# Fifteen loads moved to ScalarE's queue and a new fixed order in a recurrent-attention and maxout-FFN kernel

## The chip, the cores and the metric

The kernel runs on one core of a Trainium2 chip. A core has a matrix engine (PE, TensorE), a vector engine (DVE, VectorE), an activation engine (ACT, ScalarE), a general engine (POOL, GpSimd) and a sync engine (SP), each with its own instruction queue that runs in order. Transfers are issued by SP or ACT and carried out by 16 DMA engines. The metric is device microseconds of one execution, the median over several runs.

## The reference

Thirty-two heads (4 batches of 8) run a gated linear recurrence over 768 steps with head width 48; the result is laid out as 3072 tokens of 384 features and goes through an FFN with a maximum of three products.

```python
state = zeros(B, H, 48, 48)
for t in range(768):
    state = alpha[:, :, t, :, None] * state + einsum('bhd,bhe->bhde', k[:, :, t], v[:, :, t])
    y[:, :, t] = einsum('bhd,bhde->bhe', q[:, :, t], state)
x = y.transpose(0, 2, 1, 3).reshape(3072, 384)
h = maximum(maximum(x @ w1, x @ w2), x @ w3)      # [3072, 768]
out = h @ w_out                                   # [3072, 384]
```

Inputs and output are 32-bit; the kernel computes in 16-bit with 32-bit sums.

## The kernel before

**Tiling.** Time is cut into 6 chunks of 128 steps. One chunk of one batch is a *unit* u (24 in all, all 8 heads of 128 tokens); two units form a *group* n (12 in all). Within a unit the recurrence becomes products of matrices: logarithms of alpha (ln) are summed by a triangular product (cums), exponentials of the sums (ep, en) scale q and k (q~, k~), which are turned by PE (turn, copied back as qkT) or by a DMA transpose (cross, for the units in CROSS_Q). Scores of a unit are masked (LA), multiplied by v and added to the carried state's part (outs), scaled (xb) and turned into the FFN's layout (x turn and xT, or cross x for the units in CROSS_X). The state goes on by sums, U, G and Z.

**FFN.** max(x w1, x w2, x w3) w_out is computed as x (w1 w_out) plus max(relu(x (w2-w1)), x (w3-w1)) w_out. So w1 is cast (cast 0), turned (w1 turn) and multiplied by w_out (fold, w1o), and two differences are formed (sub 1, sub 2). For units u0 and u0+1, "grow u0 q g" is a product with difference g+1 for a part q of the 768 features, "relu" (ACT) and "max" (DVE) evict it, and "shrink m" gives the output of unit m, which is copied (ob) and stored. "zeros" are 27 products of zeros that fill PE at the start.

**Loads.** Each group has four loads (a, k, q, v) of 384 KB in runs of 192 bytes; the first four groups are loaded in halves of 192 KB, named "load x n 0" and "load x n 8". There are four buffers of each kind (LOADED), so the load of group n waits for the readers of group n-4. The four weight matrices come in two pieces each ("weights g 0" of 384 KB, "weights g 1" of 768 KB).

**The fixed order.** Nothing is scheduled while it runs. `Plan.step` (lines 135 to 157) records 801 steps with what each reads and writes, and `Plan.issue` (lines 159 to 167) emits them in the order written out in ORDER; each step goes to the first engine in its list of options, or to the second where PICK has its number. BANKS names the PSUM bank of each product's result. Since each engine runs its instructions in order, ORDER is five orders in one: the order among steps on one engine counts, and an instruction that waits holds all those behind it on its engine. SP's queue of the old order has 90 steps: 64 loads, 8 pieces of weights, 11 transposes and 7 stores; ACT's queue has 176 instructions of arithmetic and 18 stores. The options of a load stand in `load_options` (line 109), where only SP is named.

Of the kernel before, what the change touches and what calls it, by code (L numbers as in the profile page):

```python
# [35 lines left out]
    4, 5, 6, 0, 8, 9, 65, 2, 82, 1, 83, 84, 85, 10, 86, 64, 34, 88, 123, 3, 92, 89, 68, 7, 127,  # L36
    69, 94, 90, 70, 11, 71, 129, 128, 72, 32, 131, 74, 37, 91, 130, 66, 75, 133, 76, 134, 109,
    135, 35, 12, 116, 36, 136, 112, 87, 14, 56, 77, 73, 119, 132, 42, 97, 95, 106, 137, 120, 54,
    138, 78, 110, 104, 79, 33, 13, 139, 111, 80, 52, 115, 105, 121, 96, 101, 99, 93, 45, 40,
    124, 39, 81, 57, 122, 281, 44, 15, 140, 67, 98, 55, 141, 38, 102, 113, 292, 142, 103, 143,  # L40
    144, 277, 53, 288, 342, 282, 346, 289, 114, 43, 16, 117, 107, 145, 108, 20, 147, 100, 347,
    125, 148, 41, 17, 149, 293, 62, 150, 343, 60, 47, 18, 63, 146, 22, 58, 61, 278, 151, 283,
    46, 21, 126, 155, 294, 23, 59, 166, 152, 344, 48, 28, 156, 284, 279, 167, 24, 290, 168, 280,
    180, 153, 170, 345, 157, 181, 285, 154, 182, 19, 169, 158, 159, 295, 183, 233, 172, 357,
    291, 25, 163, 49, 160, 358, 296, 184, 286, 26, 173, 51, 185, 50, 161, 186, 164, 297, 174,
    162, 187, 348, 165, 175, 353, 31, 171, 195, 188, 359, 194, 30, 189, 29, 354, 176, 355, 177,
    360, 219, 190, 221, 356, 205, 178, 196, 207, 349, 118, 361, 27, 206, 191, 220, 179, 197,
    237, 192, 198, 350, 299, 209, 193, 234, 208, 415, 224, 287, 211, 416, 202, 417, 212, 222,
    235, 203, 407, 204, 418, 236, 362, 223, 199, 213, 408, 411, 300, 214, 210, 298, 225, 351,
    409, 412, 200, 413, 201, 226, 410, 263, 215, 303, 414, 238, 249, 227, 422, 264, 228, 265,  # L50
    251, 364, 267, 216, 250, 301, 323, 315, 229, 239, 253, 217, 419, 423, 218, 302, 252, 230,
    240, 317, 266, 231, 245, 255, 324, 232, 254, 365, 269, 246, 256, 241, 268, 471, 270, 247,
    325, 475, 242, 316, 248, 366, 271, 420, 243, 257, 425, 473, 272, 476, 327, 477, 368, 485,
    258, 244, 304, 273, 319, 472, 467, 478, 274, 388, 259, 318, 367, 474, 469, 260, 380, 326,
    275, 305, 261, 468, 321, 306, 262, 329, 352, 276, 369, 381, 470, 307, 530, 328, 320, 322,
    534, 370, 363, 330, 311, 531, 479, 312, 535, 308, 382, 309, 331, 390, 384, 526, 332, 310,
    427, 482, 392, 527, 333, 480, 383, 389, 426, 536, 421, 488, 313, 334, 429, 486, 537, 391,
    386, 532, 335, 387, 314, 441, 528, 533, 443, 336, 371, 338, 424, 529, 394, 339, 372, 541,
    395, 483, 489, 393, 373, 374, 396, 337, 542, 340, 442, 398, 376, 538, 487, 444, 341, 375,
    377, 448, 585, 544, 450, 397, 378, 589, 481, 385, 379, 593, 452, 590, 399, 445, 449, 430,  # L60
    403, 400, 594, 447, 451, 501, 595, 404, 431, 586, 587, 428, 596, 401, 405, 432, 591, 546,
    402, 406, 484, 588, 433, 651, 503, 592, 539, 647, 505, 502, 434, 437, 508, 648, 454, 504,
    600, 652, 506, 455, 510, 438, 507, 513, 456, 512, 548, 643, 439, 545, 458, 509, 440, 603,
    597, 543, 435, 605, 457, 644, 436, 540, 653, 601, 511, 645, 654, 446, 560, 649, 453, 646,
    561, 459, 563, 650, 490, 463, 491, 514, 604, 464, 658, 515, 460, 598, 562, 461, 516, 462,
    465, 492, 517, 567, 655, 602, 569, 466, 564, 568, 709, 571, 493, 518, 570, 547, 705, 710,
    566, 497, 607, 701, 494, 707, 706, 498, 599, 495, 573, 702, 711, 499, 708, 496, 703, 712,
    500, 519, 704, 626, 522, 520, 549, 619, 523, 627, 713, 521, 550, 628, 551, 621, 661, 630,
    524, 552, 620, 663, 556, 565, 716, 714, 662, 557, 622, 525, 553, 572, 629, 574, 656, 558,
    719, 632, 717, 575, 554, 659, 727, 555, 720, 721, 623, 576, 577, 723, 559, 625, 578, 665,  # L70
    581, 579, 725, 582, 606, 728, 664, 580, 608, 583, 729, 609, 584, 724, 610, 684, 741, 730,
    657, 745, 726, 742, 743, 722, 746, 747, 685, 744, 737, 686, 687, 748, 660, 615, 677, 734,
    688, 678, 616, 679, 690, 738, 680, 611, 633, 681, 612, 739, 634, 613, 683, 731, 614, 624,
    740, 631, 715, 636, 617, 718, 666, 635, 618, 752, 637, 667, 638, 732, 668, 689, 673, 639,
    753, 733, 749, 735, 640, 674, 641, 691, 750, 642, 675, 669, 682, 693, 755, 676, 736, 763,
    754, 670, 697, 765, 692, 671, 698, 757, 764, 672, 759, 766, 699, 694, 760, 700, 761, 695,
    756, 789, 751, 696, 758, 785, 790, 791, 762, 786, 787, 770, 788, 792, 767, 771, 773, 768,
# [685 lines left out]
```

## Time and profile before

| | |
|---|---|
| median of 3 runs | 152.29 us (152.26 to 152.42) |
| span of the profiled execution | 466.5 us |
| PE, matmuls | 1683, 457.5 us busy |
| DVE | 112.5 us busy, 196 instructions |
| ACT | 90.1 us busy, 177 instructions |
| POOL | 48.0 us busy, 72 instructions |
| DMA | 31.07 MB in 116131 packets |

The profiled execution took 466.5 us from its first to its last instruction, three times as long as the timed runs. Durations of single instructions, their order and their numbers can be read from it; which engine waits for which in the timed runs cannot be read from it directly. "PEld" is the loading of PE's weights, beside the matmuls; "SPq" and "ACTq" are the queues in which these engines issue transfers; an arrow "<-" names what ended an idle time.

### The profile page before, as it was taken

To read this page: it belongs to the slowest core of one execution; us is meant where nothing else is said; L and a number is where in the kernel's file an instruction comes from. 1 tells how busy PE (TensorE), PEld (TensorE's weight loads), DVE (VectorE), ACT (ScalarE), POOL (GpSimd) and SP (SyncE) were. 2 spreads that over 40 slices of the span, in tenths; PEclk is the share of its full clock that TensorE was granted. 3 is DMA by queue.
4 is the path that set the end of the run, shared out by engine and by line. 5 is a ranking of instruction groups with operands and counts; after the bars stand their busy time and mean duration, and the time that the engine had idled before them with its cause. 6 is when DMAs were issued, how large, how long until landed. Compare 5 with 4: busy or idle time off the path is not lost.

```text
span 466.5 us, 4171 instructions
## 1 busy us (share of the span) xinstructions
PE 457.5 (98%) x1683; PEld 263.5 (56%) x1683; DVE 112.5 (24%) x196; ACT 90.1 (19%) x177; POOL 48.0 (10%) x72
## 2 busy tenths in 40 slices
PE   4999999999999999999999999999999999999997
PEld 1667556674555656547546645545546554567473
DVE  5420313131123122222412221322221321231100
ACT  4323221122121312111212200121220111001010
POOL 0110002003001030210111120011110020000000
DMA  9999500540087000700032640020550030100001
GB/s 179 272 287 209 110 0 1 111 76 1 0 163 124 1 0 18 152 17 35 0 60 49 141 91 9 2 62 0 112 112 17 18 79 25 35 0 25 1 34 34
DMA packets 116131, 31.07 MB, mean 67 GB/s; under 512 B 109712, under 2 KB 114960, under 8 KB 116112
## 3 DMA queue, kind: packets, MB, share of 16 engines
q1 hardware_dynamic: 113232, 27.27, 27.9%
q10 hardware_dynamic: 2880, 3.54, 2.2%
q8 instruction: 13, 0.21, 0.2%
q14 instruction: 6, 0.05, 0.0%
HBM read 23.69 MB, written 4.72 MB: 61 GB/s over the span
## 4 chain that ended last, share of the span: by engine, by line
PE 98%; DMA 1%; SPq 0%; DVE 0%; issue 0%; DVEq 0%
PE psum L638 38%; PE psum L674 29%; PE psum L479 6%; PE psum L495 4%; PE psum L582 4%; PE psum L541 3%; PE psum L438 3%; PE psum L568 3%; PE psum L600 3%; PE psum L538 2%; PE psum L379 2%; DMA qn<-in_q_dram 1%; PE psum L362 1%; PE psum L408 1%; SPq L304 0%; DVE qk L450 0%
## 5 line engine op out<-in xcount | busy, mean ns | idle before, releaser
L638 PE MATMUL psum<-xT,wd 128*128 128x256 f16 (+1 forms) x540 | 186.4, 602 | 0.0
L638 PEld LDWEIGHTS <-wd 128*128 128x128 f16 x540 | 105.1, 209 | 67.5 <-issue 61.5
L674 PE MATMUL psum<-wo,hT 128*128 128x384 f16 (+1 forms) x150 | 96.7, 887 | 0.0
L674 PEld LDWEIGHTS <-hT 128*128 128x128 f16 x150 | 34.4, 230 | 54.6 <-issue 52.0
L674 PE MATMUL psum<-w1o,xT 128*128 128x384 f16 (+1 forms) x75 | 50.1, 847 | 0.0
L654 DVE TENSOR_TENSOR hT<-psum,hT 128x512 f16<-128x512 f32 (+1 forms) x39 | 24.7, 647 | 99.7 <-PE psum L638 99.7
L649 ACT ACTIVATE hT<-psum 128x512 f16<-128x512 f32 (+1 forms) x39 | 21.7, 564 | 111.0 <-PE psum L638 111.0
L500 DVE TENSOR_TENSOR LA<-psum,c 128x1024 f16<-128x1024 f32 x24 | 28.9, 1221 | 41.0 <-PE psum L495 28.7
L541 PE MATMUL psum<-v,LA 128*128 128x48 f16 x192 | 30.3, 314 | 0.0
L541 PEld LDWEIGHTS <-LA 128*128 128x128 f16 x192 | 26.5, 179 | 5.7 <-issue 5.1
L613 POOL TENSOR_TENSOR Z<-U,G 48x192 f16<-48x192 f32 x26 | 14.1, 543 | 109.5 <-DVE U L607 108.5
L438 PE MATMUL psum<-la,c 128*128 128x384 f16 x24 | 19.9, 847 | 4.3 <-ACT la L398 4.3
L479 PE MATMUL psum<-c,qk 128*128 128x128 f16 x96 | 22.1, 480 | 1.7 <-DVE qk L450 1.7
L479 PEld LDWEIGHTS <-qk 128*128 128x128 f16 x96 | 16.9, 208 | 9.1 <-DVE qk L450 4.0
L450 POOL TENSOR_TENSOR qk<-qn,ep 128x384 f16<-128x384 f32 x11 | 10.9, 994 | 105.2 <-ACT ep L443 94.0
L674 PEld LDWEIGHTS <-xT 128*128 128x128 f16 x75 | 13.1, 185 | 14.7 <-issue 14.2
L582 PE MATMUL psum<-Z 128*128 128x384 f16 x27 | 20.2, 869 | 0.0
L443 ACT ACTIVATE ep<-psum 128x384 f32<-128x384 f32 x24 | 11.7, 494 | 41.3 <-PE psum L438 41.2
L689 ACT COPY ob<-psum 128x384 f32<-128x384 f32 (+1 forms) x18 | 8.3, 469 | 54.7 <-PE psum L674 54.7
L554 DVE TENSOR_SCALAR xb<-psum,c 128x384 f16<-128x384 f32 x15 | 9.2, 617 | 37.9 <-PE psum L541 37.9
L568 PE MATMUL psum<-c,xb 128*128 128x128 f16 x63 | 17.5, 455 | 0.0
L446 ACT ACTIVATE en<-psum 128x384 f32<-128x384 f32 x24 | 11.5, 490 | 28.4 <-PE psum L438 27.1
(61 smaller groups left out, 297.2 us busy)
## 6 DMA issues: line engine op xcount, KB each, us to landing
out_dram<-ob ACTq DMA_DIRECT2D x17, 192.0 KB, 1.9
an<-in_alpha_dram SPq DMA_DIRECT2D x8, 384.0 KB, 5.3
kn<-in_k_dram SPq DMA_DIRECT2D x8, 384.0 KB, 5.4
qn<-in_q_dram SPq DMA_DIRECT2D x8, 384.0 KB, 5.7
vn<-in_v_dram SPq DMA_DIRECT2D x8, 384.0 KB, 4.2
ws<-in_moe_w_dram SPq DMA_DIRECT2D x3, 768.0 KB, 6.7
an<-in_alpha_dram SPq DMA_DIRECT2D x8, 192.0 KB, 4.0
kn<-in_k_dram SPq DMA_DIRECT2D x8, 192.0 KB, 4.0
```

The costliest lines, as they stand in the source:

```text
L438: nc.tensor.matmul(live[Lk], tri, la[:, hs, :D], start=True, stop=True)
L479: nc.tensor.transpose(live[tk][:, w, j, :], qk[:, w, 2 * j:2 * j + 2, :], ident)
L495: nc.tensor.matmul(live[Ak][:, p, j * P:(j + 1) * P], qkT[rows, 1, j, :], qkT[rows, 0, j, :], start=True, stop=True)
L500: lambda e: nc.vector.tensor_mul(LA.rearrange("p a b t -> p (a b) t"), live[Ak].rearrange("p a (b t) -> p (a b) t", t=P), maskA.unsqueeze( ...
L541: nc.tensor.matmul(yp[:, 2 * j + p, :], LA[:, p, j, :], v16[:, 2 * j + p, :], start=(cb == 0), stop=True, skip_group_check=True)
L568: nc.tensor.transpose(live[xk][:, ft, :], xb[:, ft * P:(ft + 1) * P], ident)
L582: nc.tensor.matmul(live["wm"], zero[:, :P], zero, start=True, stop=True)
L613: lambda e, rows=rows, cols=cols: engines[e].tensor_mul(Zn[rows, :, cols], (Us[u % 3] if cb else live[pk])[rows, :, cols], G[rows, i * NP: ...
L638: nc.tensor.matmul(live[gk][:, jj, :], wd[:, kt, g, j * P:(j + 1) * P], xT[:, kt, :], start=(kt == 0), stop=(kt == NFT - 1))
L649: lambda e, h=h, gk=gk: nc.scalar.activation(out=h, in_=live[gk], func=AFT.Relu),
L654: lambda e, h=h, gk=gk: nc.vector.tensor_max(h, live[gk], h),
L674: nc.tensor.matmul(live[ok][:, cols], a[:, i * P:(i + 1) * P], w[:, cols], start=(kt == 0), stop=(kt == nk - 1))
```

## The change

Loads get a second option, ACT, and a new order was written out with it: of the 801 places of ORDER 773 hold another step, of the 251 banks 215 are others, and PICK has 82 entries instead of 84. The steps themselves, their number and what they compute are the same, and PE's 273 steps keep their 1683 matmuls.

```diff
@@ ORDER, BANKS, PICK @@
 ORDER = (
-    4, 5, 6, 0, 8, 9, 65, 2, 82, 1, 83, 84, 85, 10, 86, 64, 34, 88, 123, 3, 92, 89, 68, 7, 127,
+    4, 8, 9, 5, 6, 0, 10, 12, 34, 7, 32, 1, 11, 2, 123, 65, 127, 82, 84, 128, 129, 83, 64, 131,
...
 PICK = {
-    44: 1, 71: 1, 72: 1, 75: 1, 79: 1, 81: 1, 85: 1, 86: 1, 120: 1, 131: 1, 132: 1, 145: 1, 146:
+    27: 1, 30: 1, 44: 1, 71: 1, 72: 1, 75: 1, 85: 1, 86: 1, 87: 1, 132: 1, 138: 1, 140: 1, 144:
...
 def load_options(share, n):
-    return [("SP", HARD, 0, HARD_LOAD * share, HARD_LATE * (n >= LATE_FROM))]
+    return [("SP", HARD, 0, HARD_LOAD * share, HARD_LATE * (n >= LATE_FROM)), ("ACT", 0.45, 0, HARD_LOAD * share)]
```

What the numbers come to, by the names of the steps:

- **Fifteen loads go to ACT's queue:** "v 3 0", "q 3 8", "q 4", "k 6", "v 6", "q 7", "v 7", "q 8", "a 9", "v 9", "k 10", "q 10", "v 10", "k 11" and "v 11". All stand behind the weights.
- **Stores:** six go from SP to ACT (units 0, 6, 10, 11, 20, 21) and three from ACT to SP (4, 12, 13).
- **Arithmetic:** 82 steps change their engine. Net, ACT has 7 more of them, DVE 10 fewer and POOL 3 more.
- **SP's first loads:** before a, k, q of unit 1, then a of unit 0, a and k of unit 2, q of 0, k of 0, q of 2, "weights 0 1", v of 0, 1, 2, "weights 0 0", "weights 1 1", a of unit 3, "weights 1 0", q of 3, "weights 3 1", k of 3, "weights 3 0", "weights 2 1", v of 3, "weights 2 0". After: a of unit 1, a and k of 2, k and q of 1, a of 0, q of 2, a of 3, "weights 0 1", v of 1, "weights 0 0", k of 0, v of 2, q of 0, "weights 1 0", "weights 1 1", v of 0, "weights 3 1", k and q of 3, "weights 3 0", "weights 2 1", "weights 2 0", then a of unit 4 and v of 3.
- **PE's order:** the products of one unit are spaced differently. Around unit 10 before: outs 10, turn 12, grow 8 1 1, cums 14, grow 8 0 1, x turn 10, outs 11. After: outs 11, outs 10, scores of 12 and 13, x turn 11, x turn 10.

118 rows, old and new, of tables (BANKS, ORDER, PICK) are left out of this document.

## The prediction

> **What bounds the kernel now.** I read the list of cores first, then the page (busy times, DMA, chain), then the timelines of the SP and ACT queues, the waits of SP, the groups by line, and last both orders in the code.
>
> ```profile
> core 0: 466.5 us, clock 1.000
> PE 457.5 (98%) x1683; PEld 263.5 (56%) x1683; DVE 112.5 (24%) x196; ACT 90.1 (19%) x177; POOL 48.0 (10%) x72
> PE 98%; DMA 1%; SPq 0%; DVE 0%; issue 0%; DVEq 0%
> 193.62 5.51 PE psum L674 x9
> DMA packets 116131, 31.07 MB, mean 67 GB/s; under 512 B 109712, under 2 KB 114960, under 8 KB 116112
> 20.00:50.00 30.00, 30.00 (x120) 19.92 (x118) 5.06 (x6) 9.56 (x17) 2.63 (x2) 1.00 1.07 249
> ```
>
> The profiled execution is not like the timed ones: its span is 466.5 us, the runs' median 152.29 us, a ratio of 0.326. Nine matmuls of 384 columns take 5.51 us, 612 ns each, though the granted clock reads 1.000. PE's 457.5 us must fit into 152.29, so in the runs PE is at least 3.0 times as fast, and what this profile calls hidden under PE need not be hidden there. Against the profile's own time the change is worth little: PE's 457.5 us of work stay, so its span would stay within about 1 us of 466.5 if it fell again into this rate. My sum is made for the runs. I keep the durations of DVE, ACT, POOL and DMA, which have no reason to follow PE's rate, and multiply PE's by 0.326, which is their upper bound.
>
> The Trainium skill ("TensorE: Matmul & The Clock Gate", Back-to-back issue gap) gives N/2.4 + 2.5 ns when warm: 162.5 ns for 384 columns. By it PE's work in the runs would be an estimated 121 us and 31 us of the 152 would be PE waiting; no row here shows that rate.
>
> In the runs, then, four resources are near each other: PE (at most 149 us), DVE 112.5, ACT 90.1 plus its 18 stores, and the DMA, whose 31.07 MB at the 249 GB/s of the loaded stretch are 125 us. The order is a fixed one on every engine, so the time is PE's work plus the start plus what PE waits in between.
>
> **The start.** SP's order decides when the weights are there.
>
> ```profile
> 0.74 0.46 SPq L304 DMA_DIRECT2D an<-in_alpha_dram  x1
> ...
> 25.91 1.54 SPq L323 DMA_DIRECT2D ws<-in_moe_w_dram  x1
> ```
>
> Up to this last piece of the weights ("weights 2 0") SP issues 16 half loads of 192 KB and seven pieces worth 22 such halves: 38 halves in 25.17 us, 0.66 us each. In the new order one half load fewer ("v 1 8") stands before it, so it is issued 0.66 us earlier; the pieces of matrix 0 are complete three halves earlier and those of matrix 1 one; "weights 2 1" and matrix 3 are complete at the same place, and unit 0's q and k ten halves later. The first product that needs the second difference ("grow 0 1 1") waits for "weights 2 1", which does not move; "weights 2 0" gates only the third product after it. So the gain lies between 0 and 0.66 us; I take 0.4, since the two products ahead of that gate cover only part.
>
> **Fifteen loads from SP to ACT.**
>
> ```profile
> 189.49 0.37 SPq L304 DMA_DIRECT2D vn<-in_v_dram  x1
> 190.00 1.30 SPq L304 DMA_DIRECT2D kn<-in_k_dram  x1
> 191.41 1.46 SPq L304 DMA_DIRECT2D qn<-in_q_dram  x1
> 264.58 0.34 ACTq L694 DMA_DIRECT2D out_dram<-ob  x1
> SPq L304 <- DMA out_dram<-ob: 82.7, 2, 45.9
> DMA to landing us min/median/max: 3.0/5.0/7.5
> ```
>
> The last row is that of the loads' line (L304). A load issued alone costs its queue 0.37 us; one that follows another costs 1.30 to 1.46 us, because the issue goes at the pace of the transfers. On SP this is free: nothing computes there. SP also runs far ahead of the printed order: a load goes out as soon as its buffer is free and the queue before it has passed, here behind stores. On ACT a load goes out when ACT gets to it. I counted, in the old order, the matmuls between the last thing that holds a load back on SP and its first reader: 126 to 508 for these fifteen (the least of the other late loads is "a 11" with 90). In the new order the fifteen have 45 to 189. A matmul is on average 152.29/1683 = 0.0905 us of the runs, so the shortest five have: "v 3 0" 45 = 4.1 us, "v 7" 64 = 5.8, "v 10" 65 = 5.9, "q 4" 66 = 6.0, "v 9" 68 = 6.2. Landing takes 3.0, in the median 5.0, at most 7.5 us. At the minimum none is late, at the median only "v 3 0", by 0.9 us; at the maximum all five, by 9.5 us together. Four of the five are read by ACT itself ("v 6", "v 14", "v 19", "v 21"), so a late one stops every relu, exponential and copy behind it in ACT's order. Cost: 0 to 9.5 us; a gain is excluded for these transfers, since before they had 11 us or more. I take 0.4, about half of the median case.
>
> The Trainium skill ("DMA: Bandwidth & Descriptors", Rules for kernel authors) says that spreading transfers over several issuing engines brings no bandwidth and saves only issue time. The 1.46 us of a following load, 384 KB at some 270 GB/s, agree; by it alone the term would be zero, and the 0.4 are on top of it.
>
> **Work moved between engines.** I compared the engine of every step.
>
> ```profile
> L552 ACT ACTIVATE xb<-psum,c 128x384 f16<-128x384 f32 x9 | 5.2, 581 | 53.3 <-PE psum L541 53.3
> L554 DVE TENSOR_SCALAR xb<-psum,c 128x384 f16<-128x384 f32 x15 | 9.2, 617 | 37.9 <-PE psum L541 37.9
> L573 DVE COPY xT<-psum 128x384 f16<-128x384 f16 x14 | 4.8, 356 | 38.9 <-PE psum L568 38.8
> L573 ACT COPY xT<-psum 128x384 f16<-128x384 f16 x7 | 3.3, 477 | 23.7 <-PE psum L568 23.7
> L486 ACT COPY qkT<-psum 128x1024 f16<-128x1024 f16 x5 | 5.1, 1012 | 14.3 <-PE psum L479 14.3
> L486 DVE COPY qkT<-psum 128x1024 f16<-128x1024 f16 x6 | 4.2, 692 | 30.6 <-PE psum L479 30.6
> L457 ACT ACTIVATE v<-vn,c 128x384 f16<-128x384 f32 x10 | 6.2, 617 | 0.7 <-DMA vn<-in_v_dram 0.7
> L450 DVE TENSOR_TENSOR qk<-kn,en 128x384 f16<-128x384 f32 x11 | 6.4, 598 | 11.6 <-ACT en L446 11.6
> L613 DVE TENSOR_TENSOR Z<-U,G 48x192 f16<-48x192 f32 x6 | 3.0, 493 | 0.1
> ```
>
> ACT takes, net, seven xb (+4.1 us) and four v (+2.5), and gives up three qkT (-3.0) and one xT (-0.5): +3.1 us. With fifteen loads at 0.37 (5.6 us; at most 1.46, 21.9 us) and three more stores at 0.34 (1.0), ACT goes from 96.2 us (90.1 + 18 x 0.34) to 105.9. DVE loses seven xb (-4.3), four q~ or k~ (-2.4) and three Z (-1.5), and gets one xT and three qkT (+2.4): from 112.5 to 106.7. Both are then 70% of 152.
>
> **What stands between a result and its reader.** Each PE step that reads a result of ACT or DVE is covered by the PE steps placed in between. Take outs 10, xb 10, x turn 10.
>
> ```profile
> 199.13 1.68 PE psum L495 x16
> 182.65 1.26 PE psum L568 x6
> 182.17 0.47 PE psum L438
> 182.68 0.49 ACT L443 ACTIVATE ep<-psum 128x384 f32<-128x384 f32 x1 [1.76 <-PE psum L438]
> ```
>
> In the old order turn 12, two grow of unit 8 and cums 14 lie between outs 10 and x turn 10. In the new one lie only the scores of 12 and 13 (1.68 us here, 0.55 in the runs) and x turn 11 (half of 1.26, 0.21 in the runs), 0.76 us, while xb 10 needs 0.58 us on ACT and two hand-overs; xb 11 stands before it there. I did this for all steps behind the first 20 us of PE work, with PE's rows times 0.326, the mean durations of the groups, and 0.05 us for each hand-over (ep begins 0.04 us behind the end of its sums). Nothing is negative in either order. But the three shortest spares of the new order are 0.07 (x turn 10), 0.09 (grow 14 1 0) and 0.09 us (grow 20 2 0), the shortest of the old 0.29 (grow 20 0 0). If one other instruction of 0.6 us stands ahead on the evicting engine (ACT's mean is 90.1/177 = 0.51 us, DVE's 112.5/196 = 0.57), 9 steps of the old order come late, 1.1 us together, and 19 of the new, 3.6 us. The difference, 2.5 us, is the upper end; the lower is -1.0 us, if DVE's 5.8 us less of work take waits away instead. With engines 70% busy such an instruction stands ahead in most cases, half done: I take +1.0.
>
> **Sum:** 152.29 - 0.4 (start) + 0.4 (late loads) + 1.0 (shorter cover) = 153.3 us; its own range is 152.5 (the whole start, half of the cover) to 154.2 (nothing at the start, the late load whole).
>
> **Rivals.**
>
> *DVE's relief decides* (faster). DVE was the busiest engine beside PE; with 5.8 us less on it, the waits of PE on max, LA and U get shorter. For it: DVE's 112.5 us against ACT's 96.2. Against it: the shorter spares, and ACT's 9.7 us more. It pays 1.0 us and the whole 0.66 of the start: 150.6, or 151.2 if the late "v 3 0" takes half of it back. It decides if fewer than 8 of the 19 steps meet a waiting instruction (8/19 of the 2.5 us are about its 1.0 us). I give 25%, with 151.2.
>
> *Instruction packets* (faster). PE's instructions come in packets by DMA.
>
> ```profile
> q8 instruction: 13, 0.21, 0.2%
> PEld L674 <- issue: 66.2, 172, 0.5
> ```
>
> Thirteen packets take 0.2% of 16 engines' 466.5 us, 1.15 us each. At a third of the speed PE shows no wait for them over 0.5 us; at full speed it may, above all where SP sends eight loads in a row. All of them bared would be 15 us; loads spread over two queues might save a tenth, 1.5 us, which with the start gives 150.4, and 150.8 with the late load. 12%.
>
> The Trainium skill ("Runtime: NRT & Kernel Launch", Instruction fetch mechanics) holds that a block of 256 instructions is fetched while the one before runs, mostly hidden; by it this rival would not exist and the time would stay on the other terms. Thirteen packets of 16 KB fit its blocks; no row here shows PE at full speed.
>
> *ACT held up* (slower still). The loads meet SP's transfers, cost 1.46 us instead of 0.37 on ACT (16.4 us more) and land at 7.5 us. For it: the DMA is loaded 125 of 152 us. Against it: the store at 264.58 took 0.34 us amid SP's loads. If a third of the 9.5 us reaches PE, 153.3 - 0.4 + 3.2 = 156.1; with a fifth, 154.8. I give 15%, with 155.
>
> *Nothing moves*: the loads were hidden and stay hidden, and gain and loss of the new order cancel: 152.3, 8%.
>
> **How the numbers follow.** The forecast has 40%. Slower than 152.6 (0.2% is about what three such runs can tell) are forecast and held-up ACT: 0.55. Same: 0.08. Faster: 25 + 12 = 0.37. The range goes from the packets' lower case, 150.4, to 155.6, between the two prices of a held-up ACT; the forecast's own range is the one beside its sum.
>
> **What would show it.** In the changed profile: the last weights piece issued about 0.66 us earlier; fifteen loads on ACT's queue at 0.37 us each if its ring is empty, 1.3 to 1.5 if not; ACT or v waiting for vn behind the early loads; PE waiting for xb, xT and qkT at x turn 10, grow 14 and grow 20. If PE again runs at 612 ns for 384 columns, none of the waits will show. A time below 152 means that the tight spares are not met and one of the first two rivals holds; above 155 that ACT is held up.

## The result, and the profile after

The changed kernel took 151.37 us (median of 20 runs, 149.42 to 152.43), the kernel before 151.94 us (20 runs, 151.06 to 153.46): a ratio of 0.9947, 95% interval 0.9921 to 0.9973. A second, later comparison gave 0.9855 (0.9813 to 0.9897). So it is faster, by half a per cent to one and a half; 153.3 us was forecast.

None of the later profiles shows the slow matmuls of the one read before the prediction. So from here "before" is a second and a third execution of the kernel before, with spans of 151.7 and 151.1 us. First the core, the page's busy times and the shares of the chain that ended last, of the changed kernel:

```profile
core 0: 150.3 us, clock 0.977
PE 133.8 (89%) x1683; PEld 104.5 (70%) x1683; DVE 106.1 (71%) x186; ACT 90.5 (60%) x184; POOL 52.7 (35%) x75
PE 77%; DMA 7%; ACT 6%; SPq 4%; DVE 2%; issue 1%; ACTq 0%
```

The same of the kernel before, third execution, and two pieces of its chain:

```profile
core 0: 151.1 us, clock 1.000
PE 134.0 (89%) x1683; PEld 104.5 (69%) x1683; DVE 108.7 (72%) x196; ACT 88.0 (58%) x177; POOL 49.1 (33%) x72
PE 46%; SPq 25%; DMA 19%; issue 3%; ACT 1%; DVE 1%; POOL 1%; DVEq 0%; ACTq 0%; POOLq 0%
...
98.98 0.97 PE psum L674 x6
...
108.13 5.40 DMA ws<-qk
```

Six matmuls of 384 columns take 0.97 us, 162 ns each, not 612. TensorE (PE) is busy 134 us in both kernels, so the change is not in its work but in what it waits for. In the chain of before, SP's issuing and the landing of transfers have 44%; after the change, 11%. The stretches show where. Columns: the stretch, its length, then busy time and count of PE, PEld, DVE, ACT, POOL, the granted clock, the DMA share and GB/s. Before, third execution:

```profile
0.00:30.00 30.00, 19.15 (x217) 12.92 (x218) 15.57 (x38) 17.63 (x30) 5.17 (x9) 1.00 1.03 259
90.00:120.00 30.00, 27.89 (x350) 21.89 (x348) 23.33 (x40) 16.75 (x36) 12.10 (x18) 1.00 1.11 202
```

After, a second execution (span 149.1 us):

```profile
0.00:30.00 30.00, 17.73 (x202) 12.15 (x203) 14.70 (x35) 17.73 (x32) 5.41 (x9) 0.89 1.00 254
90.00:120.00 30.00, 29.99 (x370) 23.95 (x368) 25.19 (x44) 18.63 (x40) 15.95 (x23) 1.00 1.17 213
```

The start became worse (15 matmuls fewer in the first 30 us, and a lower clock). The gain lies between 90 and 120 us: there PE of before stands still for 2.1 of 30 us, PE of after not at all. The waits of PE name the cause. Before, three of its rows (waiting engine, line, what it waited for; us in total, times, longest):

```profile
PE psum L495 <- DMA ws<-qk: 1.7, 1, 1.7
...
PE psum L495 <- DMA qkT<-qk: 0.4, 1, 0.4
...
PE psum L568 <- DVE xb L554: 0.2, 1, 0.2
```

After, second execution, all its rows:

```profile
PE psum L436 <- ACT la L396: 5.4, 1, 5.4
PE psum L360 <- ACT w1h L327: 4.9, 1, 4.9
PE psum L477 <- POOL qk L448: 0.9, 1, 0.9
PE psum L636 <- DVE wd L335: 0.9, 1, 0.9
```

All four of after belong to the start. Before has in addition waits for `ws<-qk` and `qkT<-qk`, the DMA transposes ("cross" steps) that SP issues. Its queue shows why they are late (before, third execution, SP's timeline; start, duration, transfer):

```profile
97.53 1.81 SPq L304 DMA_DIRECT2D qn<-in_q_dram  x1
99.39 2.79 SPq L304 DMA_DIRECT2D kn<-in_k_dram  x1
102.28 1.35 SPq L694 DMA_DIRECT2D out_dram<-ob  x1
103.67 0.43 SPq L304 DMA_DIRECT2D vn<-in_v_dram  x1
104.27 3.07 SPq L469 DMA_TRANSPOSE ws<-qk  x1
107.39 0.58 SPq L694 DMA_DIRECT2D out_dram<-ob  x1
108.13 2.08 SPq L469 DMA_TRANSPOSE ws<-qk  x1
```

The inputs of the second transpose (cross 19) were complete at 103.5 us; it goes out at 108.1, behind a load, a transpose and a store. It lands 5.4 us later (the last row of its chain above), and scores 18 starts late by 1.92 us. The other execution of before shows the same: issued 5.2 us behind its inputs, a stall of 1.56 us. (The stall is in the step's second half, which reads transpose 19.)

The third row is the same queue at one remove, though its name points at DVE. Load v 10, one of the fifteen, has its buffer free at 83.7 us, but on SP it stands behind transposes 21 and 20, and the inputs of transpose 20 are complete only at 113.7. So the load goes out at 120.3 and lands at 126.1 (before, third execution; timelines of SP, ACT and DVE):

```profile
120.33 3.27 SPq L304 DMA_DIRECT2D vn<-in_v_dram  x2
...
126.14 0.61 ACT L457 ACTIVATE v<-vn,c 128x384 f16<-128x384 f32 x1 [1.68 <-DMA vn<-in_v_dram]
...
130.15 1.02 DVE L689 COPY ob<-psum 128x384 f32<-128x384 f32 x2 [1.33 <-DMA out_dram<-ob]
```

ACT waits 1.68 us for it, so two stores behind on ACT go out late. The copy ob 19 on DVE waits for the second of them to free its buffer, xb 21 stands behind that copy, and x turn 21 is late by 0.39 us (1.05 in the other execution). So in SP's one queue of before a transpose waits behind loads and stores, and a load behind transposes. After the change (second execution):

```profile
95.23 2.85 SPq L302 DMA_DIRECT2D an<-in_alpha_dram  x1
103.93 2.68 SPq L467 DMA_TRANSPOSE ws<-qk  x2
106.87 1.51 SPq L559 DMA_TRANSPOSE xT<-xb  x1
```

SP is idle when the inputs come, and both transposes go out one behind the other, 0.6 and 1.1 us behind their inputs. The loads q 10, k 10 and v 9, which stood here, and both stores are in ACT's queue.

### The profile page after: what moved, and what is told of

Read it like the earlier page. It is cut to its first block, busy times and chain, and to the rows that moved or that the text cites. A ratio compares the mean times of both kernels' runs of the same rounds, so it can differ in the third digit from the quotient of the medians.

```text
span 150.3 us, 4161 instructions
## 1 busy us (share of the span) xinstructions
PE 133.8 (89%) x1683; PEld 104.5 (70%) x1683; DVE 106.1 (71%) x186; ACT 90.5 (60%) x184; POOL 52.7 (35%) x75
## 2 busy tenths in 40 slices
DMA packets 116131, 31.07 MB, mean 207 GB/s; under 512 B 109712, under 2 KB 114960, under 8 KB 116112
## 4 chain that ended last, share of the span: by engine, by line
PE 77%; DMA 7%; ACT 6%; SPq 4%; DVE 2%; issue 1%; ACTq 0%
PE psum L636 32%; PE psum L672 22%; DMA vn<-in_v_dram 4%; SPq L302 4%; PE psum L477 4%; PE psum L493 4%; DMA out_dram<-ob 3%; PE psum L539 3%; PE psum L436 3%; PE psum L536 2%; PE psum L566 2%; PE psum L598 2%; PE psum L377 2%; PE psum L406 1%; DVE wd L335 1%; ACT w1h L327 1%
## 5 line engine op out<-in xcount | busy, mean ns | idle before, releaser
L636 PE MATMUL psum<-xT,wd 128*128 128x256 f16 (+1 forms) x540 | 54.4, 251 | 0.6 <-DVE wd L335 0.6
L636 PEld LDWEIGHTS <-wd 128*128 128x128 f16 x540 | 42.9, 98 | 8.6 <-issue 2.1
L672 PE MATMUL psum<-wo,hT 128*128 128x384 f16 (+1 forms) x150 | 27.7, 320 | 0.0
L672 PEld LDWEIGHTS <-hT 128*128 128x128 f16 x150 | 14.5, 98 | 8.9
L448 POOL TENSOR_TENSOR qk<-qn,ep 128x384 f16<-128x384 f32 x11 | 10.9, 997 | 14.7 <-ACT ep L441 13.4
L672 PE MATMUL psum<-w1o,xT 128*128 128x384 f16 (+1 forms) x75 | 15.8, 320 | 0.0
L550 ACT ACTIVATE xb<-psum,c 128x384 f16<-128x384 f32 x16 | 9.1, 582 | 8.9 <-PE psum L539 6.8
L436 PE MATMUL psum<-la,c 128*128 128x384 f16 x24 | 7.8, 347 | 7.2 <-ACT la L396 5.3
L396 ACT ACTIVATE la<-an 128x384 f16<-128x384 f32 (+1 forms) x16 | 10.9, 690 | 5.4 <-DMA an<-in_alpha_dram 5.4
L539 PE MATMUL psum<-v,LA 128*128 128x48 f16 x192 | 11.1, 186 | 0.1
L539 PEld LDWEIGHTS <-LA 128*128 128x128 f16 x192 | 9.8, 98 | 0.8 <-issue 0.4
```

Of the source, the lines that this page charges most:

```text
L396: lambda e, lo=lo * H, hi=hi * H: nc.scalar.activation(out=la[:, lo:hi, :D], in_=an[:, lo:hi, :], func=AFT.Ln, scale=1.0 / CDEC),
L436: nc.tensor.matmul(live[Lk], tri, la[:, hs, :D], start=True, stop=True)
L448: lambda e, w=w, x=x, d=d: engines[e].tensor_mul(qk[:, w, :, :D], ld[x][n % LOADED][:, hs], d),
L539: nc.tensor.matmul(yp[:, 2 * j + p, :], LA[:, p, j, :], v16[:, 2 * j + p, :], start=(cb == 0), stop=True, skip_group_check=True)
L636: nc.tensor.matmul(live[gk][:, jj, :], wd[:, kt, g, j * P:(j + 1) * P], xT[:, kt, :], start=(kt == 0), stop=(kt == NFT - 1))
L672: nc.tensor.matmul(live[ok][:, cols], a[:, i * P:(i + 1) * P], w[:, cols], start=(kt == 0), stop=(kt == nk - 1))
```

## The experiments

For comparing kernels I use "lost time": the end of a step of PE less the sum of the shortest durations of it and all its steps before (121.4 us in all, without the multiplications by zero). It is given when 10 us of this work are done (the start), at 66 us, and at the end. Between 10 and 66 it shows what the first half lost, between 66 and the end the second.

| kernel | ratio to before (95%) | lost at 10 | at 66 | at the end |
|---|---|---|---|---|
| before, second and third execution | 0.9970 (0.9932-1.0009), 1.0001 (0.9966-1.0035) | 21.3, 20.9 | 23.0, 22.7 | 26.9, 26.3 |
| after, first and second execution | 0.9947 (0.9921-0.9973), 0.9855 (0.9813-0.9897) | 21.3, 21.9 | 24.9, 23.7 | 26.0, 24.7 |
| e1: after, 15 loads on SP | 1.0033 (0.9993-1.0072) | 20.8 | 24.7 | 27.3 |
| e2: before, 15 loads on ACT | 1.0062 (1.0019-1.0104) | 21.6 | 26.4 | 28.4 |
| e3: before, new start | 1.0120 (1.0055-1.0185) | 25.2 | 26.4 | 27.5 |
| e4: after, old start | 1.0261 (1.0206-1.0316) | 28.1 | 29.7 | 30.8 |
| x1: before, transposes first | 0.9947 (0.9911-0.9984) | 21.1 | 22.7 | 26.4 |
| x3: after, ob 6 first | 0.9945 (0.9902-0.9987) | 21.2 | 24.5 | 25.5 |
| x5: e2, ln 7 first | 1.0140 (1.0083-1.0198) | 21.7 | 26.8 | 28.5 |
| x7: after, PE kept warm | 1.0018 (0.9976-1.0059) | 21.0 | 24.7 | 27.6 |
| f1: after, late 10 on SP | 1.0008 (0.9963-1.0052) | 22.4 | 24.0 | 27.5 |
| f2: after, early 5 on SP | 0.9910 (0.9867-0.9952) | 21.0 | 24.3 | 25.3 |
| f3: f1 with v 7, v 9 on ACT | 0.9953 (0.9918-0.9989) | 21.3 | 23.6 | 26.4 |
| f4: after, q 7 on SP | 0.9895 (0.9855-0.9936) | 21.3 | 23.3 | 25.4 |
| x8: x1, late 10 on ACT | 1.0269 (1.0231-1.0307) | 20.4 | 22.2 | 29.8 |
| x10: x8, a 11 back | 1.0097 (1.0056-1.0138) | 21.3 | 23.0 | 27.0 |
| x9: before, late 10 and two stores on ACT | 1.0040 (0.9997-1.0084) | 20.9 | 22.4 | 25.5 |

Each ratio is against runs of the kernel before on the same chip; the chips differed (medians of before from 151.94 to 153.37 us). On one chip together ran b0, e1, e2 and e3; x1, x3, x5 and e4; a2, x7, f1 and f2; b1, x8, f3 and f4; x10 and x9. Within a chip the kernel before came out up to 0.3% from itself, and the two ratios of the changed kernel, whose intervals do not meet, are from different chips; so half a per cent between two chips says nothing. The lost times are of one execution each.

### The three parts of the change, one at a time

**b0** is the kernel before again (the second execution above). **e1** is the changed kernel with the fifteen loads back on SP:

```diff
 PICK = {
...
-    27: 1, 30: 1, 235: 1, 365: 1, 367: 1, 427: 1, 428: 1, 487: 1, 544: 1, 547: 1, 604: 1, 605: 1, 606: 1, 662: 1, 664: 1,
```

**e2** is the kernel before with the same fifteen loads on ACT, at their old places in the order (the second option of `load_options` as in the diff, and the same entries of `PICK` added). **e3** is the kernel before with the new order of SP's first 25 transfers, all else as it was:

```diff
-load a 0 8, load k 0 8, load q 0 8, load a 0 0, load a 1 0, load k 1 0, load q 0 0, load k 0 0, load q 1 0, weights 0 1,
+load a 0 8, load a 1 0, load k 1 0, load k 0 8, load q 0 8, load a 0 0, load q 1 0, load a 1 8, weights 0 1, load v 0 8,
...
```

> The kernel before, unchanged, for a profile at PE's full rate and for what two equal kernels show against each other: a ratio of 1.000 within 0.3%. Theory L (the loads on ACT's queue gave the gain): SP's loads in this profile come in longer bursts and more of PE's waits end with a transfer than in the changed kernel. Theory S (the start gave it): the last weights piece is issued 0.66 us later than the changed kernel's 24.78 us or so, and the first grow of the second difference is later by as much. Theory O (the order and the engines of the arithmetic gave it): the same stall as the changed kernel's near 72 us, where ob waits for a store, is longer or more frequent here, and DVE is 112.5 us busy against 106.1.

> The changed kernel with its fifteen loads back on SP, at the same places of ORDER; all else is the changed kernel's. Theory L: the gain is gone, ratio to the kernel before 1.000 or above (152 us). Theories S and O: the gain stays, 0.995 (151.3 us), or grows a little, to 0.993, since ACT is freed of 15 x 0.40 us.

> The kernel before with the same fifteen loads on ACT's queue, at their old places of ORDER; nothing else. Theory L: faster, ratio 0.995 (151.3 us). Theories S and O: no gain, 1.000 to 1.006, since ACT has 15 x 0.40 = 6 us more.

> The kernel before with the changed kernel's order of SP's first 25 transfers (inputs of the first groups and the weights); PE's and the other orders stay the old ones. Theory S: faster by the 0.66 us of the weights, ratio 0.9955, if the old PE order can use it; it may also lose, since the old order wants unit 1's and unit 0's inputs first, up to 1.02. Theories L and O: no gain.

None of the parts gives the gain alone. The new order with the loads on SP is not faster; the loads on ACT in the old order cost 0.6%; the new start in the old order costs 1.2%. In e1 loads now go out too late; SP's timeline of e1 has load q 4 at

```profile
53.87 1.53 SPq L300 DMA_DIRECT2D qn<-in_q_dram  x1
```

against 50.8 us on ACT in the changed kernel (second execution), and PE loses 0.56 and 0.97 us at turn 9 and totals 5. In e2 the transposes are on time, but ACT stands (its timeline):

```profile
75.55 0.50 ACT L444 ACTIVATE ep<-psum 128x384 f32<-128x384 f32 x1
78.82 0.34 ACTq L695 DMA_DIRECT2D out_dram<-ob  x1
79.21 0.84 ACT L399 ACTIVATE la<-an 128x768 f16<-128x768 f32 x1 [3.16 <-DMA an<-in_alpha_dram]
```

The store at 78.82 has its data since 64.3 us. What it waits for stands in the trace's records: the transfers of both queues share eight semaphores, and in none of the 19 profiles taken after the prediction (1,900 pairs) is a transfer issued before the one before it on the same semaphore has landed. Here that one is SP's load a 8, issued at 68.2 and landed at 78.75. Everything behind the store on ACT waits too, and cums 14 stalls 2.22 us.

### Single waits taken away

**x1** moves transposes of before ahead of loads and stores that stood in front of them. SP's sequence, by the steps' names:

```diff
-store 6, cross 14, load v 7, load q 9, cross 16,
+cross 14, store 6, load v 7, cross 16, load q 9,
...
-store 11, load v 9, cross 18, store 10, cross 19, cross x 16, load a 11, load q 11, load k 11, cross 21, cross 20,
+load v 9, cross 18, cross 19, store 11, store 10, cross x 16, cross 21, load a 11, load q 11, cross 20, load k 11,
```

**x3** swaps one pair on ACT in the changed kernel (427 is load q 7, 480 is ob 6), **x5** one on ACT in e2 (429 is ln 7, 421 is store 4), and **e4** gives the changed kernel the order of SP's first 25 transfers of before (the lines of e3 the other way round):

```diff
-    363, 427, 480, 373,
+    363, 480, 373,
...
-    376, 421, 485,
+    376, 427, 421, 485,
```

```diff
-    421, 488, 313, 334, 429,
+    429, 421, 488, 313, 334,
```

> The kernel before, with SP's transposes 14, 16, 18, 19, 20, 21 put ahead of the loads and stores that stood in front of them although the transposes' inputs were ready (up to 5.2 us earlier). Theory Q (single waits in the transfer queues make the difference: in the kernel before, TensorE's stall of 1.56 us ahead of scores 18 is transpose 19 standing behind two stores and a load on SP): the stalls ahead of scores 14 (0.50) and 18 (1.56) go, ratio to before 0.987 to 0.993. Theory A (order and engines of the arithmetic make the difference, the queues are covered): within 0.3% of before. Theory D (the transfer engines are full, so that whatever is put behind is late in turn): a new stall of 1 us or more at the store's or load's user, shrink 14 or 15, v 18 or q~ 18, and no gain.

> The changed kernel with one pair swapped on ScalarE: output copy ob 6 ahead of load q 7, which waited 3.06 us for the semaphore that load v 5 held. Theory Q (ScalarE stood in that wait, and TensorE's cums 15 behind it): cums 15's stall of 2.00 us shrinks to under 0.5, ratio to before 0.980 to 0.988 (the changed kernel had 0.995). Theory A: ScalarE has slack there, TensorE waits soon after for something else, ratio 0.993 to 0.997. A third way, that the store's landing held ob 6 (as the releaser in the profile says): ob 6 stays at 76 and the stall stays.

> The kernel before with the fifteen loads on ScalarE (which was 0.6% slower than before) and one more step moved: ln 7 ahead of store 4 on ScalarE, whose issue waited at 78.8 us for the semaphore that load a 8 held. Theory Q: the stall of 2.22 us at cums 14 goes or shrinks under 0.7, ratio to before 0.990 to 0.997, so that the loads on ScalarE give a gain in the old order as well. Theory A (the new order of the arithmetic is what lets the loads help): still 1.003 to 1.009.

> The changed kernel with SP's first 25 transfers in the order of before. Theory S (the new order of the start gives the gain): the 0.5% are lost, ratio to before 0.999 to 1.003. Theory Q: the start gives nothing (TensorE had lost 21.3 us in both kernels when 10 us of its work were done), ratio 0.993 to 0.997, or worse by a new stall later if the transfers then land in another order.

x1 is faster than before by as much as the changed kernel was in the first comparison, though by less than theory Q has. Its stall at x turn 21 is gone, but not that at scores 18 (2.34 us). The wait has another name now; of PE's waits in x1:

```profile
PE psum L495 <- ACT ob L689: 2.1, 1, 2.1
```

The copy is ob 14. Its product was complete at 109.4 us; store 10, which frees its buffer, was issued at 109.0 instead of 107.4 and begins to land at 113.0; the copy starts at 113.3, in before at 111.0. (The page's inference names another releaser, DVE's LA; the landing in the trace's records fits the time.) So what was put behind is late in its turn: theory D beside theory Q.

x3 tests the largest stall of the changed kernel's first profile, 2.00 us at cums 15 (timelines of SP, ACT and PE, all of the changed kernel):

```profile
66.92 1.71 SPq L302 DMA_DIRECT2D vn<-in_v_dram  x1
...
71.62 0.53 ACTq L692 DMA_DIRECT2D out_dram<-ob  x1
75.55 0.40 ACTq L302 DMA_DIRECT2D qn<-in_q_dram  x1
76.04 0.48 ACT L687 COPY ob<-psum 128x384 f32<-128x384 f32 x1 [3.56 <-DMA out_dram<-ob]
...
76.57 0.32 PE L436 MATMUL psum<-la,c 128*128 128x384 f16 x1 [1.84 <-ACT ob L687]
```

The profile names a store as what ended ACT's 3.56 us; the semaphore's record names load v 5, the transfer before q 7 on the same semaphore, which landed at 75.53. In x3:

```profile
73.83 0.48 ACT L687 COPY ob<-psum 128x384 f32<-128x384 f32 x1 [0.69 <-PE psum L493]
75.25 0.40 ACTq L302 DMA_DIRECT2D qn<-in_q_dram  x1
```

The copy no longer waits for any store, so the third way falls: it had stood behind q 7. The stall is gone, and yet the ratio is 0.9945, theory A's; smaller stalls stand at grow 4 (0.47), cums 16 (0.58) and totals 8 (0.28). Before cums 16, ACT waits 1.7 us at the next load, q 8, for the semaphore of k 8. x5 is worse than e2, and than both of its theories: cums 14 is on time, but now sums 8 and shrink 8 lose 2.2 us, waiting for a copy of qkT on ACT and an output copy on DVE. e4, also worse than both theories, loses everything at the start. The largest of PE's waits in it, and the largest of e3:

```profile
PE psum L360 <- ACT w1h L327: 8.6, 1, 8.6
```

```profile
PE psum L479 <- DVE qk L450: 11.0, 2, 7.6
```

Here each start order of transfers fits only the order of arithmetic that was made with it: in the changed kernel the old one costs 2.6% against before, and in before the new one costs 1.2%.

### The start's clock, and the two halves of the loads

After the change PE has nothing to do from 12.9 to 17.5 us, and its granted clock falls (windows of the changed kernel):

```profile
16.00:18.00 2.00, 0.53 (x6) 0.54 (x7) 1.10 (x2) 2.00 (x4) 0.00 (x0) 0.50 1.03 221
18.00:20.00 2.00, 2.00 (x22) 1.66 (x21) 0.02 (x1) 1.32 (x3) 0.00 (x0) 0.50 1.02 380
```

**x7** fills the gap with 24 more multiplications by zero:

```diff
-        def zeros(e):
+        def zeros(e, more=0):
             live["wm"] = bank(("wm", 0), [P, DM], FP32)
-            nc.tensor.matmul(live["wm"], zero[:, :P], zero, start=True, stop=True)
+            for _ in range(1 + more):
+                nc.tensor.matmul(live["wm"], zero[:, :P], zero, start=True, stop=True)
...
-            plan.step(f"zeros {i}", [("PE", 0.163)], 90.0, zeros,
+            plan.step(f"zeros {i}", [("PE", 0.163)], 90.0,
+                      lambda e, i=i: zeros(e, 24 if i == 20 else 0),
```

**f1** puts the ten later loads back on SP, **f2** the five early ones; **a2** is the changed kernel again:

```diff
-    427: 1, 428: 1, 487: 1, 544: 1, 547: 1, 604: 1, 605: 1, 606: 1, 662: 1, 664: 1,
```

```diff
-    27: 1, 30: 1, 235: 1, 365: 1, 367: 1,
```

> The changed kernel once more, beside its variants on one chip and for a second profile. All theories: ratio to before 0.992 to 0.998. The stall at cums 15 of 2.00 us comes again if ScalarE's wait for the semaphore of load v 5 belongs to the order; if it was one execution's chance, it is gone and another stall of its size stands elsewhere.

> The changed kernel with 24 more multiplications by zero in TensorE's gap ahead of w1 turn 2 (12.9 to 17.5 us, waiting for ScalarE's copy of the weights), so that the granted clock should not fall to 0.50 from 15.6 to 22 us, as it does in the changed kernel and not in before. Theory W (the cold stretch takes back what the new start would give): the clock reads 1.00 there, TensorE's 4.5 us of work in it take about 2.2 us less, ratio to before 0.982 to 0.990. Rival (the start is bound by the weights: the first grow waits for the difference on VectorE at 25.2 us all the same): clock 1.00, but the first grow starts within 0.3 us of 25.25, ratio 0.993 to 0.997.

> The changed kernel with ten of the fifteen loads back on SP (q 7 and all later); the early five (v 3, q 3, q 4, k 6, v 6) stay on ScalarE. With all fifteen on SP it was 0.9% slower than with none. Theory E (the early five carry the gain: on SP, q 4 went out 3.7 us later, and turn 9 and totals 5 stalled 1.53 us): ratio to before 0.993 to 0.998. Theory T (the late ten carry it, by freeing SP for the transposes): 1.001 to 1.006.

> The changed kernel with the early five of the fifteen loads (v 3, q 3, q 4, k 6, v 6) back on SP; the late ten stay on ScalarE. Theory E: ratio to before 1.001 to 1.006, with stalls near turn 9 and totals 5 again. Theory T: 0.993 to 0.998, and the transposes 18 to 23 issued soon behind their inputs. If both f1 and f2 come out between, each half carries part.

These four ran on one chip. In a2 load q 7 went out without a wait, and no stall stands at cums 15 or elsewhere: that stall was one execution's. (The ratio of a2 is better than was expected of it, and q 7 stands behind a store whose issue alone took 2.53 us.) f1 is 1.6% slower than a2: with the late ten on SP the median is 153.42 us, on ACT 151.07. f2 is 0.6% slower, but the two intervals overlap; its profile has small stalls at turn 9 (0.65) and totals 5 (1.01), the places where e1 lost. So the late ten carry most, as theory T has it. But its reason does not hold. In f1 transposes 18 and 19 are issued 0.2 and 2.1 us behind their inputs, and PE does not wait for them; the same in e1. It waits for a load (f1, timelines of SP, ACT and PE):

```profile
104.27 4.55 SPq L466 DMA_TRANSPOSE ws<-qk  x2
108.92 1.36 SPq L558 DMA_TRANSPOSE xT<-xb  x1
...
110.96 1.90 SPq L301 DMA_DIRECT2D vn<-in_v_dram  x1
...
116.95 1.12 ACT L454 ACTIVATE v<-vn,c 128x384 f16<-128x384 f32 x2 [4.34 <-DMA vn<-in_v_dram]
...
118.12 0.21 PE L538 MATMUL psum<-v,LA 128*128 128x48 f16 x2 [1.29 <-ACT v L454]
```

Load v 9 had its buffer free at 79.0 us and stands behind three transposes and load a 11 until 111.0, against 106.7 on ACT in a2; outs 18 stalls 1.44 us, grow 16 another 0.51. So in the old order transposes stand behind loads and stores, and one load, v 10, behind transposes; in the new one, with the late loads on SP, only loads stand behind transposes. The new places, with stores 10 and 11 on ACT, free the transposes; the late ten on ACT keep the loads from being late. No run moved the stores alone.

x7 kept the clock at 1.00, and the first grow came 0.4 us earlier than in the changed kernel's first execution (24.86 against 25.25), 1.0 than in a2. Yet its runs are 1.6% slower than a2's. In its profile transpose cross x 16 (`xT<-xb`) took 7.46 us to land, cums 15 stalled again 1.16 us behind load q 7, and grow 16 1.38:

```profile
PE psum L638 <- DMA xT<-xb: 1.5, 2, 1.2
```

At the start itself PE, once it is warm, next waits for load v 0 until 23.9 us, which is why the clock brings so little. So the cold stretch is not what limits the changed kernel. x7's ratio lies above both of its theories. Why a start that is a little earlier makes the rest slower in all twelve runs (152.01 us at the least, a2's median 151.07) I cannot show; it stays open.

### Which loads, and whether the old order can have the gain

**b1** is the kernel before, third execution. **x8** is x1 with the ten later loads on ACT, **f3** is f1 with v 7 (428) and v 9 (547) on ACT again, **f4** the changed kernel with q 7 alone back on SP:

```diff
+    427: 1, 428: 1, 487: 1, 544: 1, 547: 1, 604: 1, 605: 1, 606: 1, 662: 1, 664: 1,
```

```diff
+    428: 1, 547: 1,
```

```diff
-    427: 1,
```

> The kernel before once more, for a second profile. All theories: ratio 0.996 to 1.004. If the stalls at scores 18 (1.56 us) and x turn 21 (1.05) belong to the order (transpose 19 issued 5 us behind its inputs), they come again, over 1 us together; if they were one execution's chance, TensorE loses less than 2.5 us between 66 us of its work and the end (3.9 in the profile before this).

> The kernel before with two edits: SP's transposes ahead of the loads and stores (alone 0.9947) and the late ten loads on ScalarE. Theory P (transposes and loads stand in each other's way in the one queue; each edit alone moves the wait to the other kind, both together remove it): ratio to before 0.980 to 0.990, no stall over 1 us behind 66 us of TensorE's work. Theory N (it takes the new order of the arithmetic too, which leaves more time between the transposes' inputs and the scores: 8 to 9 us against 7.5 to 8): 0.993 to 1.003, with a stall of 1 us or more ahead of scores 18 again.

> The changed kernel with eight of the fifteen loads back on SP; the early five and v 7 and v 9 on ScalarE. With v 7 and v 9 on SP as well it was 1.5% slower than the changed kernel on the same chip, with stalls at outs 15 (0.40), outs 18 (1.44) and grow 16 (0.51), v 9 being issued 4 us later, behind three transposes. Theory V (these two carry the late part): stalls at outs 15 and 18 gone, ratio 0.985 to 0.992. Rival (all ten share in it, SP's queue is late as a whole): ratio 0.996 to 1.002, stalls at another load's reader.

> The changed kernel with load q 7 alone back on SP, where it went out at 69.0 us without a wait in f1. Theory Q7 (ScalarE's wait of up to 3.06 us at load q 7, seen in two of the profiles, costs the changed kernel about 1 us in the mean): ratio 0.978 to 0.986, no stall at cums 15. Rival (it is seldom or covered): 0.986 to 0.995, the same as the changed kernel.

b1 has the stalls of before again: scores 14 0.52, scores 18 1.92, x turn 21 0.39, 2.8 us together (3.1 in b0). Both later executions of this order show them. The first two are transposes (2.4 and, in b0, 2.1 us), the third is load v 10. f3 gets back about a third of what f1 had lost; the stalls at outs 15 and 18 are gone, and scores 18 stalls 1.21 us, because k 10 and q 10 are now in front of transpose 19 (PE's waits in f3):

```profile
PE psum L492 <- DMA ws<-qk: 1.0, 1, 1.0
```

That stall is the rival's, that the queue is late as a whole and which kind pays depends on which is in front; the ratio lies between the two theories. f4 is like the changed kernel, so the wait at q 7 costs little over many runs. x8 is far off both theories, and one load that x1 had moved, a 11, explains most of it (x8, ACT's timeline):

```profile
119.52 0.84 ACT L399 ACTIVATE la<-an 128x768 f16<-128x768 f32 x1 [5.35 <-DMA an<-in_alpha_dram]
```

**x10** puts a 11 ahead of transpose 21 again, and **x9** leaves the order of before untouched and takes the ten later loads and stores 10 and 11 (599, 602) to ACT:

```diff
-cross x 16, cross 21, load a 11, load q 11, cross 20,
+cross x 16, load a 11, cross 21, load q 11, cross 20,
```

```diff
+    427: 1, 428: 1, 487: 1, 544: 1, 547: 1, 604: 1, 605: 1, 606: 1, 662: 1, 664: 1,
...
-    599: 1, 602: 1,
```

> x8 with load a 11 ahead of transpose 21 again, as in before. In x8 it was issued at 113.69 us behind that transpose, landed 5.81 us later, and ScalarE's ln 11 waited for it 5.4 us, TensorE's cums 23 2.94 and grow 18 another 1.95. If that load alone made x8 slow: the stalls at cums 23 and grow 18 fall below 1 us together, ratio to before 0.990 to 1.002. If x8 is slow for another reason (many transfers in flight land late whatever their order): a stall of 2 us or more elsewhere behind 86 us of TensorE's work, ratio over 1.010.

> The kernel before, its order as it is, with the late ten loads and stores 10 and 11 on ScalarE, so that SP's transposes 18 and 19 have nothing but each other in front of them. Theory P (taking the late loads and stores off SP is the gain, in either order): ratio to before 0.985 to 0.994, no stall at scores 18. Theory N (the new order's places for them on ScalarE are part of it): 0.997 to 1.010, with a stall of ScalarE in front of one of the loads or stores that were moved, and TensorE behind it.

The place of a 11 was worth some 1.7 of the 2.7% (x8 and x10 are from two chips). x10 is still 1.0% slower than before, with stalls of 0.99 at grow 18 and 0.85 at scores 20, between the two expectations. x9 issues transposes 18 and 19 0.1 us behind their inputs or less and has no stall at scores 18. In its place scores 14 stalls 1.15 us, since transpose 14 still stands behind store 6, and scores 20 0.69; and its ratio is 1.0040, with an interval that just touches 1. Theory P falls: taking loads and stores off SP is not enough in the old order. Its profiled execution was its shortest (152.09 us, median 153.10), so where its other runs lose more than the profile shows stays open.

## Why the prediction was wrong

**The step that failed** is "On SP this is free: nothing computes there", and after it "a gain is excluded for these transfers, since before they had 11 us or more". Only what these loads cost on ACT was priced; what the queue of SP costs them, and they those behind them, was put at zero. The counts of matmuls between a load and its reader start at the last thing that holds the load back by the order; that the queue itself runs late does not enter them. SP also issues the DMA transposes, whose results PE reads 3.3 to 8.4 us after their issue in before (third execution). A load that costs its queue 1.8 or 2.8 us in front of one delays PE, however early that load itself is: scores 14 and 18 lose 2.4 us to it in the third execution of before and 2.1 in the second. Nor were the loads early. In the third execution six of the fifteen land less than 0.4 us before their reader starts (v 3 0, q 3 8, v 6, v 7, v 9 and v 10); load v 7 has its buffer free at 51.0 us and goes out at 90.0, and v 10 costs x turn 21 another 0.39 us (1.05 in the second execution). The changed kernel has none of these three stalls. What the place of the late loads is worth, with the order the same, is measured: f1 and a2 differ by 2.35 us, where the term has +0.4, a cost.

**The start**, -0.4 us: not there. Weights 2 0, forecast 0.66 us earlier than in before, went out at 24.7 us in before's third execution and 25.5 in its second, and at 25.6 and 25.3 after. But this piece did not decide the start. PE waits 4.5 and 4.9 us for the cast of matrix 0 (`w1h`), where before it waits 0.9 and 0.6 (second and third execution). The piece cast first, weights 0 1, had landed at 13.4 and 14.0 us (first and second execution), not later than in before (14.9 and 14.0), where ACT cast it at once. In the new order v 1 and three more instructions stand ahead of the cast on ACT, and v 1 waits for its load (changed kernel, first execution):

```profile
14.27 0.61 ACT L455 ACTIVATE v<-vn,c 128x384 f16<-128x384 f32 x1 [5.46 <-DMA vn<-in_v_dram]
...
15.95 1.47 ACT L327 CAST w1h<-ws 128x1536 f16<-128x1536 f32 x1
```

So the step that the forecast lacked is ACT's order: it followed the weights to SP's issue and not through the engine that casts them. Meanwhile the clock falls; the lost time at 10 us is 21.3 and 21.9 against 21.3 and 20.9. By the lost time the term is between 0 and +1.0 us. The Trainium skill ("TensorE: Matmul & The Clock Gate", Part 1: The HAM clock gate) says that the clock halves after an idle window of about 3.4 us; the gap of 4.5 us and the 0.50 behind it agree.

**Late loads on ACT**, +0.4 us: for the changed kernel their issue was sized rightly, as one row of the loads' line shows (second execution; minimum, median and maximum in ns, first and last start):

```profile
L302 ACTq DMA_DIRECT2D vn<-in_v_dram x6: 375/399/632, 46.5 to 122.1; - x6
```

No reader of v 3 0, v 7, v 9, v 10 or q 4 stalls PE. In the old order an issue on ACT could take far longer, up to 4.05 us for load a 9 in e2. What the loads do cost on ACT was not foreseen: the wait for a semaphore that another queue's transfer still holds, 3.06 us at q 7 in the first execution, none in the second. The Trainium skill's rule on spreading transfers, told in the prediction ("DMA: Bandwidth & Descriptors", Rules for kernel authors), agrees as to bandwidth: 31.07 MB, and a DMA share of 1.00 to 1.17 in the stretches shown of both kernels. But "only issue time" was not small here: issues and waits behind one another in one queue held back what PE needs, 2.8 and 3.1 us of it in before.

**Shorter cover**, +1.0 us: not there. x turn 10, grow 14 and grow 20 show no stall over 0.25 us in either execution of the changed kernel, though PE's rate left even less time between result and reader than the 0.326 allowed (162 ns a matmul where it had 200). To reckon every near neighbour on a 70% busy engine as a delay was the error.

**The rivals.** "DVE's relief decides" came out on the right side with the right size (151.2), for the wrong reason, so that is luck: DVE lost 2.6 us (108.7 to 106.1), not 5.8, and e1, which has all of that relief, is not faster than before. The one wait named after DVE's xb, at x turn 21, comes from a late load. Instruction packets: thirteen in both kernels, no stall of PE named after them. "ACT held up" is seen at q 7, but f4 shows it to be small over many runs. The range held, because it reached to the rivals' times.

The reason shown: in before PE waits in the second half for transposes that stand behind loads and stores in SP's one queue, and for a load that stands behind transposes; the late ten loads on ACT, together with the new places and the moved stores, remove both. Shown too: neither the order (e1) nor the loads (e2, x9) nor the start (e3) does it alone. Not shown: the share of the two moved stores, and of the 82 steps of arithmetic that changed their engine, which no run moved alone; why hand-made versions in the old order stay above x1's 0.9947, and what of x7's loss is chance. No version measured beats the changed kernel for certain; x3, f2 and f4 cannot be told from it.

## What to carry to other kernels

Ask of a queue that "computes nothing" what stands in it for a busy engine: compare the time at which a transfer's inputs were complete with the time at which it was issued, and do this for transposes as well as for loads. When loads move to an engine that also computes, look at what each issue may have to wait for there. In a kernel whose DMA is full, one moved transfer makes another late, so judge such an edit by many runs of the whole, not by the stall it removes: of the removals of a seen wait here, x1 and x10 gained, x3, x9 and f4 brought nothing that can be told, and x5 lost.

## What the runs showed of the hardware

One execution of the kernel before ran PE at 612 ns for 384 columns with a granted clock of 1.000; all later profiles show 162 to 163 ns, so a clock of 1.000 does not prove PE's full rate. A load's issue kept SP 0.9 to 1.3 us in the median, by kernel, and up to 4.8 us (load a 7 in the changed kernel), and ACT some 0.40 us in the median but up to 4.05 us (load a 9 in e2). And the semaphores of transfers tie the two queues to each other: ACT stood up to 3.06 us in the changed kernel, and 3.16 in e2, because a load of SP had not landed.
